# Loading q, k and v as fp32 from the SP queue and casting them on chip, in a windowed attention with a gated FFN behind it

## The chip, the core and the metric

The kernel runs on one core of a Trainium2 chip. Its engines run side by side, each with an instruction stream of its own that it works through in order: PE multiplies matrices, DVE and ACT do elementwise work, Pool does elementwise work too and also issues transfers, and SP does nothing but issue transfers. A transfer that Pool issues can change the type of the data on the way; here, one issued by SP or ACT leaves it as it is. The metric is the time of one execution in microseconds, the median of several runs. One further execution is taken with the profiler, and the views below are of that one.

## The reference

Attention with four sink keys and a window of 128, for 4 batches, 8 heads, 768 positions and head size 64, and behind it an FFN with a gate (512 to 1536 to 512) over all 3072 tokens:

```python
scores = scale * np.matmul(q, k.transpose(0, 1, 3, 2))
keep = (pos[None, :] < 4) | ((rel >= 0) & (rel < 128))      # rel = query - key
a = softmax(np.where(keep, scores, -1e9))
x = np.matmul(a, v).transpose(0, 2, 1, 3).reshape(B * S, H * D)
out = (np.maximum(x @ w_gate, 0.0) * (x @ w_val)) @ w_out
```

## The kernel before

**Tiling.** Work is cut by unit: one batch `b` and one pair of heads `p`, 16 units. The 768 keys of a unit lie in seven tiles of 128 partitions that begin at the rows of `ROW0`. Tiles 1, 3 and 5 carry the four sink keys in their first four partitions, so that the scores of a query need two neighbouring tiles only; tile 6 holds the last 16 rows. q lies in six tiles of 128 rows.

**Loads.** `load_kv` (L87) and `load_q` (L83) issue one transfer a tile from the Pool queue, for both heads at once, and the transfer casts fp32 to bf16 on the way into `kn`, `vn` and `qn`; the sinks are small transfers of their own (L94). A full unit is 26 transfers. There are four slots of these tiles. The weights come in eleven transfers, also from Pool (`load_w`, `load_wo`).

**Stages of a unit.** `st_T` transposes q and k on PE (13 transposes), and DVE, ACT and DVE copy the results out to `qz` and `kT`. `st_S` multiplies scores of one of three column groups, G0, G1 and G2; ACT takes the exponential, DVE multiplies with a 0/1 mask (L170). `st_V` multiplies with v in two parts (rows 0 to 379 and 380 to 767 of the queries), with a row of ones for the denominators, and ACT copies to `oab`. `norm` (L211) sends the denominators to DRAM, back as a dense tile `dc`, through DVE's reciprocal to `dr`, to DRAM again and back, broadcast over 64 partitions, as `R`: four transfers on the SP queue, each of which waits for the one before. Two DVE products with `R` (L233, L234) write the FFN's input `xT`. Steps of `norm` are put off: `tick` counts them down, once after each stage of the prologue and once in each chunk of the FFN.

**The FFN.** `chunk` (L241) makes one of 12 column blocks of the hidden layer for half a batch: four matmuls with `wg`, ACT's relu, four with `wv`, DVE's product to `hT`. `ffn2` (L258) is one of 12 accumulating matmuls of an output tile; ACT copies the tile out, SP stores it.

**Order.** It is written out by hand. The prologue (L274 to L311) loads the first three tiles of batch 0's four units, sets up masks and slots, and runs T, G0, G1a, V part 0 and `norm` of these halves. Then come 8 blocks of 12 chunks (two blocks a batch; the first has 380 columns). Between the chunks the list `stages` is worked off: first the second halves of batch 0, then the 12 full units of batches 1 to 3, T, V part 1 of the unit before, G0, G1, G2, V part 0. `want` (L372) sets how many stages have been issued by each chunk: 2.5 a chunk for 17 chunks, one a chunk after. A unit's loads are issued 11 stages ahead of its T (L357). Three `ffn2` of the block before follow each chunk.

**Buffers.** gp and vp share three PSUM buffers, T, S and V share two (`ps_at`), output tiles have one.

## Time and profile before

| | us |
|---|---|
| median of two runs (463.24 and 463.99) | 463.62 |
| the profiled execution | 466.86 |
| its span, first to last instruction | 465.0 |
| busy in it: Pool | 349.6 |
| PE | 292.8 |
| DVE | 143.7 |
| ACT | 140.8 |

Busy time is summed over the span's instructions of an engine; overlapping matmuls count once. "Pool DMA_DIRECT2D" is the time that Pool takes to issue a transfer, not the transfer's own. In a line of the chain or a timeline the first column is the start in us from the span's start, the second the duration. In a group's line stand count, busy us and mean ns of one, then the idle time of the engine just before and what ended it. A line of windows has: stretch, length, then busy time and count of PE, PE's weight loads, DVE, ACT and Pool, the granted PE clock, the share of time in which the DMA engines were busy, and GB/s.

### The profile page before, as it was taken

What the parts mean: (1) busy time and instruction counts of PE and PEld (TensorE: products, weight loads), DVE (VectorE), ACT (ScalarE), POOL (GpSimd) and SP (SyncE); (2) the same over time, 40 slices, a digit from 0 to 9 for tenths busy, and PEclk for the clock granted to TensorE, in tenths of its full rate; (3) what the DMA queues carried; (4) which work ended last, traced back from release to release, by engine and by line L of the source; (5) the groups of instructions that cost most, each with busy time, mean ns of one, the idle gap of its engine ahead of it and who ended that gap; (6) DMA issues with size and microseconds to landing.
All of it is one profiled execution on the core that took longest, in us unless ns stands there. A gap on an engine that the chain in (4) does not pass through costs nothing.

```text
span 465.0 us, 5011 instructions
## 1 busy us (share of the span) xinstructions
PE 292.8 (63%) x1752; PEld 170.9 (37%) x1752; DVE 143.7 (31%) x280; ACT 140.8 (30%) x225; POOL 349.6 (75%) x439
## 2 busy tenths in 40 slices
PE   0033320564062818254959798897969699999996
PEld 0022110342031505132535354554536365555552
DVE  0721012342022413051624433254334334422220
ACT  1022200353022405051515242433525253233332
POOL 8999499995999999999999999999999400000000
PEclk9999999988557676695979897989889799999999
DMA  4468975659556565756586775768585521110102
GB/s 26 23 33 85 203 63 52 43 45 151 40 33 63 33 66 27 67 42 53 27 90 77 60 88 51 85 45 102 26 90 50 79 52 27 61 47 23 47 23 90
DMA packets 171632, 27.79 MB, mean 60 GB/s; under 512 B 161084, under 2 KB 167756, under 8 KB 171608
## 3 DMA queue, kind: packets, MB, share of 16 engines
q0 software_dynamic: 160944, 14.61, 47.5%
q1 hardware_dynamic: 10664, 12.88, 9.9%
q8 instruction: 13, 0.21, 0.2%
q14 instruction: 11, 0.09, 0.1%
HBM read 34.96 MB, written 6.49 MB: 89 GB/s over the span
## 4 chain that ended last, share of the span: by engine, by line
POOL 61%; PE 23%; DMA 9%; issue 6%; ACT 0%; POOLq 0%; ACTq 0%
POOL vn L92 20%; POOL kn L92 17%; POOL qn L85 13%; PE op L265 8%; PE gp L246 7%; PE vp L252 7%; POOL vn L94 5%; POOL kn L94 4%; DMA kn<-in_k_dram 3%; DMA wo<-in_moe_w_out_dram 2%; DMA qn<-in_q_dram 2%; DMA vn<-in_v_dram 1%; PE ops L181 1%; POOL wg L99 1%; POOL wv L99 1%
## 5 line engine op out<-in xcount | busy, mean ns | idle before, releaser
L92 POOL DMA_DIRECT2D kn<-in_k_dram x112 | 107.4, 968 | 10.5 <-DMA wo<-in_moe_w_out_dram 4.8
L92 POOL DMA_DIRECT2D vn<-in_v_dram x112 | 107.0, 960 | 1.5 <-DMA wg<-in_moe_w_gate_dram 1.1
L144 PE MATMUL tps<-ident,qn 128*128 128x128 bf16 x96 | 23.0, 263 | 126.6 <-DMA qn<-in_q_dram 115.3
L252 PE MATMUL vp<-xT,wv 128*128 128x384 bf16 (+2 forms) x384 | 86.5, 352 | 1.2 <-ACT gs L249 1.2
L246 PE MATMUL gp<-xT,wg 128*128 128x384 bf16 (+2 forms) x384 | 85.7, 349 | 0.0
L265 PE MATMUL op<-wo,hT 128*128 128x512 bf16 x288 | 80.1, 396 | 0.0
L254 DVE TENSOR_TENSOR hT<-gs,vp 128x384 bf16<-128x384 f32 (+2 forms) x96 | 52.4, 547 | 66.9 <-PE vp L252 66.2
L85 POOL DMA_DIRECT2D qn<-in_q_dram x96 | 69.6, 744 | 1.8 <-DMA vn<-in_v_dram 1.1
L152 ACT COPY kT<-tps 128x896 bf16<-128x896 bf16 (+2 forms) x20 | 15.1, 756 | 183.4 <-DVE qz L151 183.4
L144 PEld LDWEIGHTS <-qn 128*128 128x128 bf16 x96 | 9.5, 101 | 142.9 <-DMA qn<-in_q_dram 140.8
L249 ACT ACTIVATE gs<-gp 128x384 f32<-128x384 f32 (+2 forms) x96 | 47.2, 491 | 39.3 <-PE gp L246 38.8
L169 ACT ACTIVATE ee<-sps 128x1014 bf16<-128x1014 f32 (+3 forms) x52 | 45.6, 899 | 25.3 <-PE sps L166 25.2
L252 PEld LDWEIGHTS <-wv 128*128 128x128 bf16 x384 | 40.3, 105 | 31.5 <-issue 9.8
L166 PE MATMUL sps<-qz,kT 128*128 128x255 bf16 (+4 forms) x232 | 31.6, 268 | 23.7 <-DVE qz L151 17.1
L246 PEld LDWEIGHTS <-wg 128*128 128x128 bf16 x384 | 37.2, 103 | 23.3 <-issue 3.7
L170 DVE TENSOR_TENSOR ee<-ee,msk 128x1014 bf16<-128x1014 bf16 (+3 forms) x52 | 31.7, 614 | 39.5 <-ACT ee L169 39.4
L181 PE MATMUL ops<-ee,vn 128*128 128x252 bf16 (+5 forms) x256 | 32.8, 278 | 17.1 <-DVE dr L223 9.2
L151 DVE COPY qz<-tps 64x768 bf16<-64x768 bf16 (+1 forms) x20 | 9.3, 465 | 100.5 <-PE tps L147 100.4
L184 ACT COPY oab<-ops 65x760 f32<-65x760 f32 (+1 forms) x32 | 25.4, 794 | 47.8 <-PE ops L181 47.8
L265 PEld LDWEIGHTS <-hT 128*128 128x128 bf16 x288 | 29.3, 102 | 27.6 <-issue 4.3
L181 PEld LDWEIGHTS <-vn 128*128 128x128 bf16 x256 | 25.6, 116 | 28.7 <-issue 12.8
L166 PEld LDWEIGHTS <-kT 128*128 128x128 bf16 x232 | 22.1, 106 | 36.0 <-DVE qz L151 17.3
(40 smaller groups left out, 163.5 us busy)
## 6 DMA issues: line engine op xcount, KB each, us to landing
out_dram<-ot SPq DMA_DIRECT2D x24, 256.0 KB
R<-rcp_tmp SPq DMA_DIRECT2D x12, 384.0 KB
qn<-in_q_dram POOLq DMA_DIRECT2D x96, 32.0 KB, 2.5
kn<-in_k_dram POOLq DMA_DIRECT2D x48, 32.0 KB, 2.4
vn<-in_v_dram POOLq DMA_DIRECT2D x48, 32.0 KB, 2.5
wg<-in_moe_w_gate_dram POOLq DMA_DIRECT2D x4, 384.0 KB, 9.5
wv<-in_moe_w_val_dram POOLq DMA_DIRECT2D x4, 384.0 KB, 10.7
wo<-in_moe_w_out_dram POOLq DMA_DIRECT2D x3, 512.0 KB, 8.0
```

Of the source, the lines that this page charges most:

```text
L85: nc.gpsimd.dma_start(out=qn[slot][:, t, :, :], in_=rows(q, b, p, t * 128, 128))
L92: nc.gpsimd.dma_start(out=dst[lo:hi, j, :, 0:64], in_=rows(x, b, p, r0 + lo, hi - lo))
L94: nc.gpsimd.dma_start(out=dst[0:4, j, :, 0:64], in_=rows(x, b, p, 0, 4))
L144: nc.tensor.transpose(ps[:, 0, t * 128:(t + 1) * 128], qn[s][:, t, :, :].rearrange("p h d -> p (h d)"), ident[:])
L166: nc.tensor.matmul(out=ps[:, h, c0:c1], lhsT=kT[s][:, j, :], rhs=qz[s][:, h, q0:q0 + c1 - c0], start=True, stop=True)
L169: nc.scalar.activation(e, ps[:, :, lo:hi], Act.Exp, bias=0.0, scale=scale)
L181: nc.tensor.matmul(out=ps[:, h, o0:o0 + c1 - c0], lhsT=vn[s][:, j, h, :], rhs=ee[s][:, gi, h, c0:c1], start=i == 0, stop=i == len(segs) - ...
L246: nc.tensor.matmul(out=gp[:, 0:n], lhsT=wg[:, ko, m * 128:(m + 1) * 128], rhs=x[:, ko, c0:c0 + n], start=ko == 0, stop=ko == KO - 1)
L249: nc.scalar.activation(gs[:, 0:n], gp[:, 0:n], Act.Relu, bias=0.0, scale=1.0)
L252: nc.tensor.matmul(out=vp[:, 0:n], lhsT=wv[:, ko, m * 128:(m + 1) * 128], rhs=x[:, ko, c0:c0 + n], start=ko == 0, stop=ko == KO - 1)
L254: nc.vector.tensor_tensor(hT[:, m, c0:c0 + n], gs[:, 0:n], vp[:, 0:n], op=Alu.mult)
L265: nc.tensor.matmul(out=op, lhsT=hTs[b][:, m, t * 128:(t + 1) * 128], rhs=wo[:, m, :], start=m == 0, stop=m == FM - 1)
```

## The change

- **Loads.** q, k and v are loaded as fp32 into `kf`, `vf` and `qf`, two slots each. A `Unit` issues one transfer per head for k, for q and for v, with all its key tiles in one (they begin 124 rows apart now, so one access pattern covers them and the sinks aren't loaded apart), and one each for the last 24 rows of k and v: eight transfers for a full unit. They are issued from SP; the v of the first halves of batch 0 from ACT. Weights stay on Pool.
- **q's order.** A partition takes `qn` neighbouring rows of q instead of one row of each tile; T's copies to `qz` write with a step of `qn` elements to undo it.
- **Casts.** `cast` copies fp32 to bf16 on chip, with the copies of the sink rows: k, q and v of a unit on Pool, except that k and q of batch 0's first halves are cast on DVE. The `sink` tile keeps batch 0's sink rows for its second halves.
- **Batch 0.** Its units are half units: `P0` (queries 0 to 375) in the prologue, `P1` behind. Two first halves share a slot. There are two slots instead of four in all.
- **Stride.** Key tiles begin every 124 rows; the cuts of the groups and of V move with it (376 and 392 queries instead of 380 and 388), and the masks are built anew.
- **norm.** Its four transfers are put off one by one (`s1` to `s4`), each by one `tick`.
- **Order.** A unit's cast is issued in the second stage of the unit before, its load in the fourth stage of the unit three before. Four stages (`PRE`) are issued ahead of the first chunk; after that two stages a chunk for 18 chunks, then one.

S and V are the same but for offsets. The core of the diff:

```diff
-ROW0 = [0, 124, 252, 376, 504, 628, 752]
-QCUT = 380
+QCUT = 376
...
-    SL = 4
+    kf = [const.tile([128, 7, 2, 64], F32, name=f"kf{i}") for i in range(2)]
+    vf = [const.tile([128, 7, 2, 64], F32, name=f"vf{i}") for i in range(2)]
+    qf = [const.tile([128, 6, 2, 64], F32, name=f"qf{i}") for i in range(2)]
+    sink = const.tile([4, 2, NP, 2, 64], BF16, name="sink")
...
-    def load_q(b, p, ts, slot):
-        for t in ts:
-            nc.gpsimd.dma_start(out=qn[slot][:, t, :, :], in_=rows(q, b, p, t * 128, 128))
-    def load_kv(b, p, js, slot):
-        for x, dst in ((k, kn[slot]), (v, vn[slot])):
-            for j in js:
-                r0 = ROW0[j]
-                lo, hi = (4, 128) if j in (1, 3, 5) else ((0, 16) if j == 6 else (0, 128))
-                nc.gpsimd.dma_start(out=dst[lo:hi, j, :, 0:64], in_=rows(x, b, p, r0 + lo, hi - lo))
-                if j in (1, 3, 5):
-                    nc.gpsimd.dma_start(out=dst[0:4, j, :, 0:64], in_=rows(x, b, p, 0, 4))
...
+    class Unit:
+        def __init__(self, i, b, p, half):
+            self.i, self.b, self.p, self.half, self.s = i, b, p, half, i % 2
+            if half == 0:
+                self.js, self.q0, self.n, self.qn, sub = (0, 1, 2), 0, QCUT, 3, p // 2
+                self.jo, self.qo, self.zo = 3 * sub, 3 * sub, 384 * sub
+                self.qrows, self.qp = 384, 128
+            elif half == 1:
+                self.js, self.q0, self.n, self.qn = (2, 3, 4, 5, 6), QCUT, S - QCUT, 4
+                self.jo, self.qo, self.zo = 0, 0, 0
+                self.qrows, self.qp = S - QCUT, 98
+            else:
+                self.js, self.q0, self.n, self.qn = tuple(range(7)), 0, S, 6
+                self.jo, self.qo, self.zo = 0, 0, 0
+                self.qrows, self.qp = S, 128
+            self.j5 = [j for j in self.js if j < 6]
+            self.a, self.e = self.jo + self.j5[0], self.jo + self.j5[-1] + 1
+        def load(self, eng=None, veng=None):
+            eng, veng = eng or nc.sync, veng or eng or nc.sync
+            s, a, e = self.s, self.a, self.e
+            for en, x, dst in ((eng, k, kf[s]), (eng, q, qf[s]), (veng, v, vf[s])):
+                for h in range(2):
+                    src = x[self.b, 2 * self.p + h]
+                    if x is q:
+                        r = src[self.q0:self.q0 + self.qrows, :].rearrange("(p n) d -> p n d", n=self.qn)
+                        en.dma_start(out=dst[0:self.qp, self.qo:self.qo + self.qn, h, :], in_=r)
+                        continue
+                    r = bass.AP(src.tensor, src.offset + 124 * self.j5[0] * D,
+                                [[D, 128], [124 * D, e - a], [1, D]])
+                    en.dma_start(out=dst[:, a:e, h, :], in_=r)
+                if x is not q and 6 in self.js:
+                    en.dma_start(out=dst[0:24, 6, :, :],
+                                 in_=x[self.b, 2 * self.p:2 * self.p + 2, 744:768, :].rearrange("h s d -> s h d"))
+        def cast(self, what, eng):
+            s, a, e = self.s, self.a, self.e
+            cp = eng.tensor_copy
+            if what == "q":
+                cp(qn[s][0:self.qp, self.qo:self.qo + self.qn, :, :].rearrange("p j h d -> p (j h d)"),
+                   qf[s][0:self.qp, self.qo:self.qo + self.qn, :, :].rearrange("p j h d -> p (j h d)"))
+                return
+            w = 0 if what == "k" else 1
+            src, dst = (kf[s], kn[s]) if w == 0 else (vf[s], vn[s])
+            if w == 0:
+                cp(dst[:, a:e, :, :].rearrange("p j h d -> p (j h d)"),
+                   src[:, a:e, :, :].rearrange("p j h d -> p (j h d)"))
+            else:
+                cp(dst[:, a:e, :, 0:64], src[:, a:e, :, :])
+            if 6 in self.js:
+                cp(dst[0:24, 6, :, 0:64], src[0:24, 6, :, :])
+            if self.half == 0:
+                cp(sink[:, w, self.p, :, :], src[0:4, a, :, :])
+            for j in (1, 3, 5):
+                if j in self.js:
+                    cp(dst[0:4, self.jo + j, :, 0:64],
+                       sink[:, w, self.p, :, :] if self.half == 1 else src[0:4, self.jo, :, :])
+        def T(self):
+            s, nq = self.s, self.qn
+            ps = ps_at.tile([128, 2, 1024], BF16, name="tps", tag="at")
+            w = self.qp * nq
+            po = ps[:, 0, 0:w].rearrange("d (n p) -> d n p", n=nq)
+            for t in range(nq):
+                nc.tensor.transpose(po[:, t, :], qn[s][0:self.qp, self.qo + t, :, :].rearrange("p h d -> p (h d)"),
+                                    ident[0:self.qp, 0:self.qp])
+            for j in self.js:
+                nc.tensor.transpose(ps[:, 1, j * 128:(j + 1) * 128],
+                                    kn[s][:, self.jo + j, :, :].rearrange("p h d -> p (h d)"), ident[:])
+            z0 = self.zo + self.q0
+            d0, d1 = self.js[0], self.js[-1] + 1
+            zq = [qz[s][64 * h:64 * h + 64, h, z0:z0 + w].rearrange("d (p n) -> d n p", n=nq) for h in range(2)]
+            nc.vector.tensor_copy(zq[0], po[0:64])
+            nc.scalar.copy(kT[s][:, self.jo + d0:self.jo + d1, :].rearrange("p j n -> p (j n)"),
+                           ps[:, 1, d0 * 128:d1 * 128])
+            nc.vector.tensor_copy(zq[1], po[64:128])
...
+    def norm(b, p, oab, q0, n, d):
         cc = 12 if n == S else 8
         pp = 2 * n // cc
+        dd, rr = den_d[b, p, 2 * q0:2 * (q0 + n)], rcp_d[b, p, 2 * q0:2 * (q0 + n)]
         dc = dpool.tile([128, 12], F32, name="dc")
         dr = dpool.tile([128, 12], F32, name="dr")
+        R = []
+        def s1():
+            nc.sync.dma_start(out=dc[0:pp, 0:cc], in_=dd.rearrange("(p c) -> p c", c=cc))
+            after(d, s2)
+        def s2():
             nc.vector.reciprocal(dr[0:pp, 0:cc], dc[0:pp, 0:cc])
             nc.sync.dma_start(out=rr.rearrange("(p c) -> p c", c=cc), in_=dr[0:pp, 0:cc])
+            after(d, s3)
+        def s3():
+            R.append(rpool.tile([64, 2, S], F32, name="R"))
+            nc.sync.dma_start(out=R[0][:, :, 0:n], in_=rr.rearrange("(h s) -> h s", h=2).partition_broadcast(64))
+            after(d, s4)
+        def s4():
+            x = xTs[b]
+            busy.discard(next(i for i in range(4) if oab_[i] is oab))
+            ready[b, p] = q0 + n
+            for h in range(2):
+                nc.vector.tensor_tensor(x[64 * h:64 * h + 64, p, q0:q0 + n], oab[0:64, h, q0:q0 + n],
+                                        R[0][:, h, 0:n], op=Alu.mult)
+        nc.sync.dma_start(out=dd.rearrange("(o h s) -> o h s", o=1, h=2), in_=oab[64:65, :, q0:q0 + n])
+        after(d, s1)
...
+        for u in P0:
+            u.load(nc.sync, nc.scalar)
...
+        def cast0(u):
+            u.cast("k", nc.vector)
+            u.cast("q", nc.vector)
+            u.cast("v", nc.gpsimd)
+        def V0(p):
+            o = new_oab()
+            P0[p].V(0, o)
+            norm(0, p, o, 0, QCUT, 1)
+        cast0(P0[0])
+        P0[0].T()
+        cast0(P0[1])
+        P0[1].T()
+        for p in range(NP):
+            P0[p].S("G0")
+            tick()
+            P0[p].S("G1a")
+            tick()
+            if p + 2 < NP:
+                cast0(P0[p + 2])
+                if p == 0:
+                    load_w(0)
+                P0[p + 2].T()
+                if p == 1:
+                    P1[0].load()
+                    P1[1].load()
+            if p >= 1:
+                V0(p - 1)
+            if p == 2:
+                P1[0].cast("k", nc.gpsimd)
+                P1[0].cast("q", nc.gpsimd)
+                load_w(1)
+            if p == 3:
+                P1[0].cast("v", nc.gpsimd)
+            tick()
+        V0(NP - 1)
+        casts(P1[1], nc.gpsimd)
+        P1[2].load()
...
+        def unit_stages(x):
+            u = rest[x]
+            prev = rest[x - 1] if x else None
+            nxt = rest[x + 1] if x + 1 < len(rest) else None
+            nxt3 = rest[x + 3] if x + 3 < len(rest) else None
+            def first():
+                if u.half is None and u.p == 0:
+                    newx(u.b)
+                u.T()
+            yield first
+            if prev is not None:
+                def second():
+                    V_(prev, 1)
+                    if nxt is not None and x >= 1:
+                        casts(nxt, nc.gpsimd)
+                yield second
+            if u.half is None:
+                yield lambda: u.S("G0")
+            yield lambda: u.S("G1" if u.half is None else "G1b")
+            def fourth():
+                u.S("G2")
+                if nxt3 is not None:
+                    nxt3.load()
+            yield fourth
+            if u.half is None:
+                yield lambda: V_(u, 0)
+        for x in range(len(rest)):
+            stages += list(unit_stages(x))
...
+        PRE = 4
+        while si < PRE:
+            stages[si]()
+            si += 1
+            tick()
+        while not all(ready.get((0, p), 0) >= QCUT for p in range(NP)):
+            tick()
         for bi, (b, c0, n) in enumerate(blocks):
             if c0 == 0:
                 hTs[b] = hpool.tile([128, FM, S], BF16, name="hT")
             for m in range(FM):
                 ci = bi * FM + m
-                want = (ci + 1) * 5 // 2 if ci < 17 else 42 + (ci - 16) * 24 // 24
+                want = PRE + (ci + 1) * 2 if ci < 18 else PRE + 38 + (ci - 18)
```

234 lines of the change are left out of this document (74 added, 160 removed), and 8 rows, old and new, of the table SEG.

## The prediction

> **What bounds the kernel now.** I read the page first (span, slices, shares of the chain of waits, costliest groups), then the chain itself, then timelines of PE, SP and DVE, and windows.
>
> ```profile
> span 465.0 us, 5011 instructions
> POOL 8999499995999999999999999999999400000000
> POOL 61%; PE 23%; DMA 9%; issue 6%; ACT 0%; POOLq 0%; ACTq 0%
> L92 POOL DMA_DIRECT2D kn<-in_k_dram x112 | 107.4, 968 | 10.5 <-DMA wo<-in_moe_w_out_dram 4.8
> ```
>
> Pool is full for 31 of 40 slices, it holds 61% of the chain, and what it does is write descriptors: 0.97 us for each small transfer of k, and v and q are loaded the same way. The chain shows the cadence this gives:
>
> ```profile
> 40.34 0.77 POOL wg L99
> ...
> 127.00 4.34 POOL qn L85 x6
> ...
> 148.10 4.34 POOL qn L85 x6
> ...
> 365.18 2.42 DMA qn<-in_q_dram
> ...
> 453.00 8.43 PE op L265 x39
> ```
>
> The q loads of successive units start 21.1 us apart (127.00, 148.10): a unit (one batch, one pair of heads) costs Pool 21.1 us, and twelve of them 253 us. The last q lands at 367.6; only the 97.4 us behind it are PE's own. What PE needs when nothing is late is read where Pool is done:
>
> ```profile
> 375.45 0.60 PE L166 MATMUL sps<-qz,kT 128*128 128x255 bf16 x4
> 375.89 0.81 PE L246 MATMUL gp<-xT,wg 128*128 128x384 bf16 x4
> 376.54 0.81 PE L252 MATMUL vp<-xT,wv 128*128 128x384 bf16 x4
> 377.19 0.81 PE L265 MATMUL op<-wo,hT 128*128 128x512 bf16 x3
> ...
> 380.22 0.54 PE L166 MATMUL sps<-qz,kT 128*128 128x255 bf16 x6
> 380.61 0.81 PE L246 MATMUL gp<-xT,wg 128*128 128x384 bf16 x4
> ...
> 382.56 0.71 PE L181 MATMUL ops<-ee,vn 128*128 128x255 bf16 x6
> 383.11 0.81 PE L246 MATMUL gp<-xT,wg 128*128 128x384 bf16 x4
> ...
> 385.05 0.88 PE L181 MATMUL ops<-ee,vn 128*128 128x127 bf16 x10
> 385.79 0.81 PE L246 MATMUL gp<-xT,wg 128*128 128x384 bf16 x4
> ```
>
> From start to start (matmuls overlap, so the durations don't add): gp 0.65, vp 0.65, a G0 or G1 0.44, a G2 0.39, a V part 0 0.55, a V part 1 0.74. One output matmul is 8.43 / 39 = 0.216 us. Transposes, and the first FFN chunk, in the earlier part of the PE timeline:
>
> ```profile
> 87.23 1.47 PE L246 MATMUL gp<-xT,wg 128*128 128x380 bf16 x4
> ...
> 95.83 0.33 PE L144 MATMUL tps<-ident,qn 128*128 128x128 bf16 x3
> 96.00 0.39 PE L147 MATMUL tps<-ident,kn 128*128 128x128 bf16 x4
> 96.22 1.05 PE L181 MATMUL ops<-ee,vn 128*128 128x127 bf16 x10
> ```
>
> Seven transposes take 0.39 us: 0.056 each.
>
> **PE's whole work from the first chunk on.** 96 chunks x 1.30 = 124.8; 288 output matmuls x 0.216 = 62.2; 12 full units x (13 x 0.056 + 0.44 + 0.44 + 0.39 + 0.55 + 0.74 = 3.29) = 39.5; four second halves of batch 0 x (9 x 0.056 + 0.44 + 0.39 + 0.74 = 2.07) = 8.3. Together 234.8; four stages (1.8 us) now run ahead of the first chunk, so 233. The new stride changes column counts by under 3%: nothing.
>
> **The first chunk's start.** Before it is 87.2 us. Pool's setup no longer stands behind descriptors:
>
> ```profile
> 12.19 0.25 DVE L121 COPY msk<-msk 128x12 bf16<-128x12 bf16 x1 [12.19 <-POOL msk L113]
> ...
> 15.02 0.38 DVE L134 MEMSET qz<- 64x384 uint32 x1
> ...
> 17.12 0.38 DVE L134 MEMSET qz<- 64x384 uint32 x1
> ```
>
> ```profile
> L170 DVE TENSOR_TENSOR ee<-ee,msk 128x1014 bf16<-128x1014 bf16 x28 | 19.4, 692 | 26.7 <-ACT ee L169 26.7
> L233 DVE TENSOR_TENSOR xT<-oab,R 64x768 bf16<-64x768 f32 x12 | 11.4, 950 | 25.5 <-DMA R<-rcp_tmp 25.5
> L111 POOL TENSOR_SCALAR_AFFINE_SELECT msk<-msk 128x252 bf16<-128x252 bf16 x1 | 0.4, 397 | 0.1
> masks.py:199 POOL TENSOR_SCALAR_AFFINE_SELECT ident<-ident 128x128 bf16<-128x128 bf16 x1 | 0.3, 287 | 0.1
> ```
>
> Eight setup operations at no more than 0.40 end at about 3.6 us; DVE's mask work takes 2.8 (12.19 to 15.02), a slot 2.1 (15.02 to 17.12), and there are two slots now: DVE is free at 3.6 + 2.8 + 4.2 = 10.6, and its first casts and the first transposes follow. Before, it took 4.7 us from the last unit's loads (wg starts at 40.34) to that chain's first denominator store (45.06, below). Four half units, one after the other at 4.7, put the first store at 10.6 + 18.8 = 29.4; I take 30, between 20 (two of them hidden) and 45 (as now). From there the order on SP decides:
>
> ```profile
> 45.06 0.71 SPq L217 DMA_DIRECT2D den_tmp<-oab  x1
> ...
> 60.93 0.61 SPq L217 DMA_DIRECT2D den_tmp<-oab  x1
> ...
> 68.01 0.59 SPq L217 DMA_DIRECT2D den_tmp<-oab  x1
> ...
> 79.21 0.62 SPq L226 DMA_DIRECT2D R<-rcp_tmp  x1
> ...
> 381.03 0.34 SPq L270 DMA_DIRECT2D out_dram<-ot  x1
> ```
>
> SP runs its transfers in order, so one pair's store, load, store, broadcast ends before the next pair's begins: 7.1 us a pair (60.93 to 68.01), 11.2 for the last two (to 79.21), 8.0 to the first chunk (87.23). After: 30 + 2 x 7.1 + 11.2 + 8.0 = 63.4. The loads of batch 0's second halves now stand between these on SP: eight each, at 0.34 each at least (the out row, 128 pieces) 2.7 us, mostly in SP's waits: 64. Bounds 53 (from 20) and 87.
>
> **Loads.** The 26 Pool transfers of a unit become eight on SP: (6 x 128 x 2 + 48) x 2 + 6 x 128 x 2 = 4704 rows of 256 bytes.
>
> ```profile
> q0 software_dynamic: 160944, 14.61, 47.5%
> q1 hardware_dynamic: 10664, 12.88, 9.9%
> ```
>
> No row shows such a transfer. From below: q1's time per byte, 0.099 x 465 x 16 / 12.88 MB = 57 us a MB, is 15 ns a row. From above: all of q0's time on its 74,752 rows of q, k, v (counted from the loops) is 47 ns. I take 20, near q1: the same kind of queue, without a cast. A unit's load is then 4704 x 20 / 16 = 5.9 us of the engines (4.3 to 13.8). SP's issue of one is between 0.34 and six times that, 2.0 (768 pieces against 128); I take 0.7, so 5 us a unit. In the steady part a unit has six chunks of 1.30 + 0.65 and its own 3.29: 15.0 us. The load stands behind that unit's four norm transfers, and the next denominator store comes three stages, 7.5 us, later. Both fit: no cost. If not, what is late next is the denominator, see the first rival.
>
> The Trainium skill (DMA: Bandwidth & Descriptors, Specifications) speaks against this: below 512 bytes a transfer does a read-modify-write and misses line rate. If I price that as twice the bytes' 15 ns, an estimate, a unit's load is 8.8 us, over the 7.5, and the sum grows by 1.3 x 12 = 16 us.
>
> **Casts on Pool.** Three of 768 elements and eight small ones a unit. Bounds from the two affine_select rows: 0.89 ns an element (397 less 287, over 124) and 0.17 fixed. Big 0.85, small 0.29: 3 x 0.85 + 8 x 0.29 = 4.9 us; from 1.9 (fixed only) to 7.8 (twice the slope for fp32). The casts are issued four stages before the transposes that read them, some 10 us: hidden, so Pool costs nothing. A cast waits for its load and for V of the unit two back; SP's load three units ahead waits for the cast that frees its fp32 tile, and behind it on SP stand the next denominators and out stores. DVE's qz copies write with a step: at worst 0.95, the 768-element row, hidden by the two chunks before G0.
>
> **Stalls.** Two stages a chunk run in the first 18 chunks. Windows:
>
> ```profile
> 87.00:111.00 24.00, 17.98 (x137) 11.62 (x136) 8.78 (x19) 12.81 (x20) 23.63 (x30) 0.93 0.71 74
> 380.00:410.00 30.00, 28.84 (x176) 16.42 (x175) 12.31 (x21) 11.20 (x21) 0.00 (x0) 1.00 0.22 62
> ```
>
> In the first, of this kind, PE idles 25%; the part after holds about 47 us of PE work, so 47 x 24 / 17.98 - 47 = 16 at most, partly waits on loads: I take 10. The second idles 4%: over some 136 us of steady work 5.5. The end, last matmul to end of span, is 465.0 - 461.4 = 3.6.
>
> **Sum.** 64 + 233 + 10 + 5.5 + 3.6 = 316 us of span. The profiled execution took 466.86 for its span of 465.0 (+1.9), and stands 3.2 above the median of 463.62: about 315.
>
> **Rivals.**
> - *SP and the DMA rings take Pool's place.* At 47 ns a row, or 2.0 us an issue, a load lasts 13 us, 5.5 more than the 7.5 until the next denominator. DVE waits in order for it at the reciprocal, behind it the mask and hT products, then PE. 5.5 x 12 = 66: 381. For it: one SP queue now carries everything. Against: q1 shows 15 ns for the bytes.
> - *Pool's casts hold up DVE.* Five DVE products a unit read two SBUF tiles (rows L170, L233). If each waited for one 0.85 us cast and nothing hid it, 5 x 0.85 x 12 = 51: 366; half of them, 341. No row shows Pool reading while DVE multiplies. The Trainium skill (SBUF — State Buffer, Who interferes with whom) states that a Vector instruction with two SBUF inputs contends with a GpSimd one that reads SBUF, under an exclusive lock. Against: DVE has slack in each chunk.
> - *Slower: the casts are as dear as the descriptors.* One mechanism: Pool stays the bound when a unit's casts exceed (473 - 64 - 28 - 97) / 12 = 23.7 us, with 28 for batch 0's second halves and 97 for the end as before. At 25 us it gives 489. It needs five times my 4.9; then the change would not do what it says, and just under it is no change.
> - *All hidden.* First chunk at 53 and no early stalls: 315 - 11 - 10 = 294; I count it with the forecast.
>
> **How the numbers follow.** Forecast 0.67 (own range 285 to 345), SP and rings 0.19, Pool against DVE 0.08, casts too dear 0.04, casts just under that 0.02. Range 285 to 355: it leaves out the first rival's upper two thirds (0.13) and the last two (0.06). 2% is about what a measurement can tell: faster 0.94, within 2% 0.02, slower 0.04.
>
> **What would show it.** Pool's slices fall to some 3 tenths; the chain is PE after the first chunk; gp begins near 64; SP's den to dc stays near 2 us in the steady part. Wrong if DVE's waits on dc grow past 5 us a unit, if Pool casts exceed 2 us, or if PE waits for kn or qn casts.

## The result, and the profile after

The changed kernel takes 390.44 us (median of two runs, 390.11 to 390.76) for 463.62 before: a ratio of 0.842, with an interval of 0.838 to 0.846. The forecast was faster, 315 us with a range of 285 to 355: the direction holds, the size does not, 75 us are missing. In the tables below, the ratios leave out executions that took over 1.5% more than the fastest of their kernel, the medians do not (two of four with the old row order and weights late, one of four with the old row order and R from Pool).

The page of the changed kernel: span, Pool's row of the forty slices, the queue that now carries the loads, the chain that ended last by engine.

```profile
span 388.4 us, 5029 instructions
POOL 6240531307424304311404040404010000000000
q1 hardware_dynamic: 87208, 31.91, 37.5%
PE 48%; DVE 24%; DMA 11%; ACT 6%; issue 4%; SPq 4%; POOL 1%; DVEq 0%; ACTq 0%; POOLq 0%
```

Pool was busy through 31 slices and held 61% of the chain; now it is mostly idle and holds 1%. That bound is gone. But DVE, absent from the chain before, has 24% of it. The groups by line, shapes kept apart, of DVE, and its waits and PE's over the whole run:

```profile
L156 DVE COPY qz<-tps 64x768 bf16<-64x768 bf16 x12 | 32.7, 2724 | 11.7 <-ACT kT L154 11.7
L153 DVE COPY qz<-tps 64x768 bf16<-64x768 bf16 x12 | 32.6, 2714 | 3.5 <-PE tps L148 3.5
```

```profile
PE sps L164 <- DVE qz L156: 39.5, 17, 5.7
DVE xT L287 <- DMA R<-rcp_tmp: 34.1, 14, 6.9
```

A copy of 768 columns of q from PSUM to `qz` takes 2.72 us, and PE waits 39.5 us for the second of the two before it can multiply scores. Windows (width, then busy time of PE, PEld, DVE, ACT and Pool, granted clock, DMA share, GB/s) by part:

```profile
98.00:171.00 73.00, 47.99 (x325) 30.67 (x322) 54.98 (x57) 30.38 (x43) 22.96 (x57) 0.80 0.53 114
191.00:313.00 122.00, 108.77 (x745) 65.39 (x744) 82.62 (x96) 58.25 (x94) 18.92 (x49) 0.98 0.41 88
313.00:385.00 72.00, 70.63 (x392) 37.90 (x389) 20.39 (x37) 22.50 (x45) 0.00 (x0) 1.00 0.13 47
```

PE idles 2% of the last stretch, 11% of the steady part with one stage a chunk, and 34% of the part with two stages a chunk. Ahead of these the FFN's first matmul comes at 79.0 us (first start in the row of its tile), where 64 was forecast:

```profile
L301 PE MATMUL gp<-xT,wg x384: 319/326/534, 79.0 to 375.4; 128*128 128x384 bf16 x144, 128*128 128x376 bf16 x24, 128*128 128x392 bf16 x24
```

So three places are to be explained: the copies, the prologue, and the part with two stages a chunk. PE's granted clock, 0.80 in the first of these windows, comes back in the account of the prediction.

### The profile page after: what moved, and what is told of

Read it like the earlier page. It is cut to its first block, busy times and chain, and to the rows that moved or that the text cites. A ratio compares the mean times of both kernels' runs of the same rounds, so it can differ in the third digit from the quotient of the medians.

```text
span 388.4 us, 5029 instructions
## 1 busy us (share of the span) xinstructions
PE 272.5 (70%) x1760; PEld 163.6 (42%) x1760; DVE 207.7 (53%) x286; ACT 141.3 (36%) x225; POOL 83.2 (21%) x203
## 2 busy tenths in 40 slices
DMA packets 96241, 37.74 MB, mean 97 GB/s; under 512 B 85692, under 2 KB 92364, under 8 KB 96216
## 4 chain that ended last, share of the span: by engine, by line
PE 48%; DVE 24%; DMA 11%; ACT 6%; issue 4%; SPq 4%; POOL 1%; DVEq 0%; ACTq 0%; POOLq 0%
PE vp L307 14%; PE op L320 13%; PE gp L301 12%; DVE qz L153 10%; DVE qz L156 8%; PE sps L164 6%; DMA kf<-in_k_dram 4%; ACT kT L154 3%; DMA R<-rcp_tmp 3%; DMA dc<-den_tmp 2%; DVE xT L287 2%; PE ops L176 2%; ACT ee L167 2%; SPq L109 2%; SPq L111 1%
## 5 line engine op out<-in xcount | busy, mean ns | idle before, releaser
L307 PE MATMUL vp<-xT,wv 128*128 128x384 bf16 (+2 forms) x384 | 83.2, 342 | 14.2 <-ACT gs L304 14.2
L164 PE MATMUL sps<-qz,kT 128*128 128x251 bf16 (+5 forms) x232 | 35.3, 293 | 47.8 <-DVE qz L156 39.5
L167 ACT ACTIVATE ee<-sps 128x1006 bf16<-128x1006 f32 (+4 forms) x52 | 46.1, 900 | 53.2 <-PE sps L164 53.2
L168 DVE TENSOR_TENSOR ee<-ee,msk 128x1006 bf16<-128x1006 bf16 (+4 forms) x52 | 33.8, 651 | 39.4 <-ACT ee L167 38.8
L287 DVE TENSOR_TENSOR xT<-oab,R 64x768 bf16<-64x768 f32 (+2 forms) x40 | 33.2, 830 | 34.4 <-DMA R<-rcp_tmp 34.1
L128 POOL CAST vn<-vf 128x768 bf16<-128x768 f32 (+2 forms) x20 | 14.7, 732 | 165.8 <-PE ops L176 163.1
L156 DVE COPY qz<-tps 64x768 bf16<-64x768 bf16 (+2 forms) x20 | 40.0, 2000 | 17.1 <-ACT kT L154 17.1
L176 PE MATMUL ops<-ee,vn 128*128 128x248 bf16 (+6 forms) x256 | 28.6, 255 | 25.8 <-DVE ee L168 18.1
L153 DVE COPY qz<-tps 64x768 bf16<-64x768 bf16 (+2 forms) x20 | 39.8, 1990 | 7.3 <-PE tps L148 7.2
L179 ACT COPY oab<-ops 65x752 f32<-65x752 f32 (+1 forms) x32 | 25.4, 795 | 25.5 <-PE ops L176 25.3
L145 PE MATMUL tps<-ident,qn 128*128 128x128 bf16 (+1 forms) x100 | 9.8, 236 | 18.5 <-DVE qn L119 18.3
L324 ACT COPY ot<-op 128x512 f32<-128x512 f32 x24 | 14.1, 587 | 22.2 <-PE op L320 22.2
```

The source lines that it names most:

```text
L153: nc.vector.tensor_copy(zq[0], po[0:64])
L156: nc.vector.tensor_copy(zq[1], po[64:128])
L164: nc.tensor.matmul(out=ps[:, h, c0:c1], lhsT=kT[s][:, self.jo + j, :], rhs=qz[s][:, h, self.zo + q0:self.zo + q0 + c1 - c0], start=True, s ...
L167: nc.scalar.activation(x, ps[:, :, lo:hi], Act.Exp, bias=0.0, scale=scale)
L168: nc.vector.tensor_tensor(x, x, msk[:, gi, :, lo:hi], op=Alu.mult)
L176: nc.tensor.matmul(out=ps[:, h, o0:o0 + c1 - c0], lhsT=vn[s][:, self.jo + j, h, :], rhs=ee[s][:, gi, h, c0:c1], start=i == 0, stop=i == le ...
```

## The experiments

Times are medians on the chip; a ratio is to the kernel before, run beside it, with its interval.

| kernel | us | ratio |
|---|---|---|
| changed kernel | 390.4 | 0.842 (0.838 to 0.846) |
| q in the old row order | 362.2 | 0.779 (0.777 to 0.781) |
| copies that read with the step | 365.9 | 0.785 (0.779 to 0.791) |
| weights late | 390.8 | 0.843 (0.839 to 0.847) |
| old row order, weights late | 361.3 | 0.772 (0.769 to 0.774) |
| Pool's large casts twice | 396.2 | 0.854 (0.851 to 0.856) |
| kernel before with the stepped copies | 465.9 | 1.000 (0.998 to 1.003) |
| old row order, R from Pool | 362.7 | 0.782 (0.776 to 0.787) |
| old row order, weights early | 355.5 | 0.764 (0.759 to 0.768) |
| read with the step, weights early | 364.9 | 0.783 (0.778 to 0.788) |
| read with the step, weights early, R from Pool | 362.5 | 0.778 (0.773 to 0.784) |
| read with the step, weights early, loads behind R | 372.7 | 0.800 (0.793 to 0.807) |

The rest, on the old row order with early weights (355.5), stand in the last part below.

### The stepped copies

**q in the old row order.** The copies write in one piece again; nothing else moves.

```diff
-  r = src[self.q0:self.q0 + self.qrows, :].rearrange("(p n) d -> p n d", n=self.qn)
+  r = bass.AP(src.tensor, src.offset + self.q0 * D, [[D, self.qp], [self.qp * D, self.qn], [1, D]])
...
-  zq = [qz[s][64 * h:64 * h + 64, h, z0:z0 + w].rearrange("d (p n) -> d n p", n=nq) for h in range(2)]
+  zq = [qz[s][64 * h:64 * h + 64, h, z0:z0 + w] for h in range(2)]
...
```

> The changed kernel with one part undone: q is loaded with neighbouring rows in neighbouring partitions, as before, in the same number of transfers and of 256-byte pieces, so that DVE's two copies to qz write without a step. Theory A (the stepped copies, 2.72 us each where 0.95 was the assumed worst, hold up DVE, G0 and the hT products behind them): the copies fall to about 0.55 us, PE's waits on qz before G0 (5 to 6 us a unit in the part with two stages a chunk) go, and the time falls by 35 to 55 us, to 335 to 355. Theory B (transfers in one another's way on SP and the DMA engines): the copies get shorter but the time falls by no more than 8 us, to 382 or more. Theory C (Pool's casts late, or in DVE's way): no more than 8 us either.

362.2 us: 28 less, short of the 35 to 55, but the largest single gain of all runs on complete kernels. One of its two copies (0.55 us; the other takes 0.56), and its windows:

```profile
L154 DVE COPY qz<-tps 64x768 bf16<-64x768 bf16 x12 | 6.5, 546 | 1.9 <-PE tps L149 1.9
```

```profile
92.00:175.00 83.00, 56.57 (x418) 37.70 (x421) 44.28 (x71) 36.90 (x55) 33.36 (x74) 0.89 0.63 128
175.00:290.00 115.00, 109.91 (x763) 68.63 (x776) 57.95 (x99) 59.99 (x97) 19.34 (x49) 0.99 0.45 96
290.00:355.00 65.00, 64.06 (x350) 34.67 (x355) 18.22 (x32) 20.10 (x39) 0.00 (x0) 1.00 0.13 47
```

In the steady part PE now idles 4%, as forecast. The part before it still idles 32%: that loss has another cause.

**The kernel before with the stepped copies.** q comes in the changed kernel's row order, still by Pool's transfers, and the copies write with the step; everything else is as before.

```diff
...
+  r = rows(q, b, p, ts[0] * 128, 128 * n).rearrange("(p n) h d -> p n h d", n=n)
+  nc.gpsimd.dma_start(out=qn[slot][:, t, :, :], in_=r[:, t - ts[0]])
...
+  zq = [qz[s][64 * h:64 * h + 64, h, c0:c1].rearrange("d (p n) -> d n p", n=nq) for h in range(2)]
...
```

> The kernel before with the stepped copies alone: q is loaded in the changed kernel's row order, and DVE puts the transposed columns back in order with copies that write with a step; all else, Pool's loads too, is as before. Theory A (the dear copies are what the changed kernel loses): each copy of 768 columns takes 2.7 us here too instead of 0.55, but Pool's descriptor writing, 21 us a unit, still sets the pace, so DVE's extra 4 to 6 us a unit is hidden: ratio 0.995 to 1.015. Rival: the copies are dear only where Pool casts beside them (the two hold one another up at the SBUF port): 0.55 to 0.95 us each here.

```profile
L158 DVE COPY qz<-tps 64x768 bf16<-64x768 bf16 x12 | 32.7, 2721 | 11.7 <-ACT kT L157 11.7
```

The same 2.72 us, with no cast on Pool, and the time does not change: a ratio of 1.0004. The copies are dear by themselves, and under the old bound they were free. Their 28 us in the changed kernel exist only because Pool no longer covers them.

**Copies alone.** Each form three times, with zeros stored as output ahead of them.

> No part of the reference is computed: copies of 64 x 768 bf16 alone, each form three times, on DVE: PSUM to SBUF with writes 1, 2, 3, 4, 6, 8, 12 and 16 elements apart; in the kernel's form with 2, 3, 4 and 6 tiles; a stepped read of PSUM with a write in one piece; a stepped write from SBUF; the same on ACT. From the changed kernel's rows, an element costs about 1.8, 2.4 and 3.4 ns at 6, 8 and 12 bytes apart. Theory by lines (a dear step whenever the next element lies in another 16-byte line): the cost is level from 16 bytes on, about 3.6 us a copy at 8, 12 and 16 elements apart; 4 bytes apart about 1.0 us. Theory by extent (the cost grows with the bytes passed over): 4.6 ns an element at 16 bytes, 9 ns at 32: 3.6, 5.3 and 7.1 us at 8, 12 and 16 elements apart. A write in one piece with a stepped read: 0.55 us if only the write side is dear, 2.7 if both are. ACT: as DVE if the port is the reason; 0.7 to 0.9 us if DVE alone is.

Groups by line of this run (the lines 55 to 69 are writes 1, 2, 3, 4, 6, 8, 12 and 16 elements apart; 77 is the kernel's own form with six tiles, 79 reads PSUM with the step and writes in one piece, 81 writes with the step from SBUF, 83 and 85 are ACT with a step of 6 and without):

```profile
L65 DVE COPY dst<-ps 64x768 bf16<-64x768 bf16 x3 | 10.6, 3542 | 0.1
L67 DVE COPY dst<-ps 64x768 bf16<-64x768 bf16 x3 | 10.5, 3509 | 0.1
L69 DVE COPY dst<-ps 64x768 bf16<-64x768 bf16 x3 | 10.0, 3350 | 0.1
L83 ACT COPY das<-ps 64x768 bf16<-64x768 bf16 x3 | 8.1, 2699 | 0.1
L63 DVE COPY dst<-ps 64x768 bf16<-64x768 bf16 x3 | 8.1, 2695 | 0.1
L77 DVE COPY dst<-ps 64x768 bf16<-64x768 bf16 x3 | 8.1, 2695 | 0.1
...
L61 DVE COPY dst<-ps 64x768 bf16<-64x768 bf16 x3 | 5.5, 1846 | 0.1
...
L81 DVE COPY dst<-sb 64x768 bf16<-64x768 bf16 x3 | 4.3, 1434 | 0.1
L59 DVE COPY dst<-ps 64x768 bf16<-64x768 bf16 x3 | 4.3, 1424 | 0.1
...
L57 DVE COPY dst<-ps 64x768 bf16<-64x768 bf16 x3 | 3.0, 1005 | 0.1
...
L79 DVE COPY dst<-ps 64x768 bf16<-64x768 bf16 x3 | 2.8, 949 | 0.1
L85 ACT COPY das<-ps 64x768 bf16<-64x768 bf16 x3 | 2.4, 792 | 0.1
L55 DVE COPY dst<-ps 64x768 bf16<-64x768 bf16 x3 | 1.6, 550 | 1.0 <-PE ps L53 0.9
```

From 4 to 12 bytes apart the price grows by (2695 - 1005) / 8 = 211 ns for a byte; at 16 it is 3542, and at 24 and 32 no more. Theory by lines fits these rows, theory by extent (7.1 us at 32 bytes) falls. The Trainium skill (SBUF — State Buffer, Specifications (TRN2)) states that SBUF has lines of 16 bytes, wants two hits or more a line for full speed, and that each cross to a new line pays; the level above 16 bytes agrees, but here the price grows from 4 to 6 to 8 bytes apart (1005, 1424 and 1846 ns), where a line still takes two hits or more, and the measurement decides. The rise from 550 to 1005 may be a matter of its own, for a stepped read that is written in one piece takes 949 too; these rows don't tell the two apart. At 12 bytes ACT pays as much as DVE.

**Copies that read with the step.** The changed kernel with the step on the other side: PSUM is read with it, `qz` is written in one piece.

```diff
-  zq = [qz[s][64 * h:64 * h + 64, h, z0:z0 + w].rearrange("d (p n) -> d n p", n=nq) for h in range(2)]
-  nc.vector.tensor_copy(zq[0], po[0:64])
+  zq = [qz[s][64 * h:64 * h + 64, h, z0:z0 + w].rearrange("d (p n) -> d p n", n=nq) for h in range(2)]
+  pr = po.rearrange("d n p -> d p n")
+  nc.vector.tensor_copy(zq[0], pr[0:64])
...
```

> The changed kernel with one expression turned round: the q copies write in one piece and read PSUM with the step (0.95 us in the run of copies alone, against 2.70). Loads, casts and order are the changed kernel's. Theory A: the same as with q in the old row order (362.2 us), or better by what the larger pieces of q save on the rings (1.5 KB instead of 256 B): 352 to 364, ratio 0.76 to 0.785. Rival (the old row order helped in another way than through the copies): 375 to 391.

```profile
L154 DVE COPY qz<-tps 64x768 bf16<-64x768 bf16 x12 | 11.4, 946 | 3.4 <-PE tps L148 3.4
```

365.9 us, a little over the 352 to 364 expected, with copies of 0.95 us: 25 of the 28 by an edit that leaves the loads alone, so it is the copies and not the row order. (The expectation's larger pieces do not exist: the page counts 96242 packets here and 96241 with the old row order.)

**Pool's casts.** Each large cast on Pool is done twice.

> The changed kernel with every large cast on Pool done twice (the second copy writes the same values again): some 2.5 us more Pool time in each full unit, 43 us over the span with the half units. Theories A and B: Pool is hidden, and the time stays within 1% of 390. Theory C: if Pool's casts were on the path, each full unit would grow by up to 2.5 us, 30 us in all, to about 420; a part of that if they only get in the way of DVE's products with two inputs in SBUF.

Pool's busy time grows from 83.2 to 124.6 us, the kernel's by 5.7 (ratio 0.854 for 0.842). Some six sevenths of the added casts are hidden. The rest is a little more than the 1% of theories A and B and far less than the 30 us of theory C, which is no main cause. What the casts do hold up is DVE's products with two inputs in SBUF: the largest of the mask products (128x1006) takes 0.955 us on average, 0.744 in the changed kernel; the copies from PSUM take 2.72 to 2.73 in both.

### The weights in the prologue

In the changed kernel DVE waits 14.1 us, until 70.9, for the way back of a denominator, while the last weights and a half unit's loads are under way. **Weights late** puts `load_w(2)` and `load_w(3)` behind the casts of the second stage of P1's second unit, and `load_wo` a unit later; the second kernel does this on the old row order.

> The changed kernel with the last seven weight transfers moved: the two last quarters of wg and wv are issued by Pool behind the casts in the second stage of the second half unit, wo behind those of the third; nothing else is changed. Theory B (the seven weight transfers, issued together at 47 to 52 us, stand in front of the loads of batch 0's third second half and of the denominators of the last two pairs, for which DVE waits 14.1 us at a reciprocal): that wait falls to about 2 us, the first FFN chunk starts at 64 to 69 instead of 79 us, and the time falls by 9 to 14 us, to 376 to 381. Theory A: the chunks' part is bound by the stepped copies and takes 306 us again; it says nothing of the prologue. Theory C: no change.

> Both edits together: q's old row order and the weights issued later. Theories A and B, each for its own part of the span, make the two gains add up: 35 to 55 and 9 to 14 us, a time of 322 to 346. If one cause lay behind both, the sum would fall clearly short of the two single gains.

No gain on the changed kernel: 390.8 us. On the old row order it is 361.3 for 362.2, by the ratios (0.772 for 0.779) some 3 us; neither is the 9 to 14 us expected. The timeline of DVE with late weights shows the wait gone from one place and come back at another (the bracket is the wait before the instruction):

```profile
57.48 0.20 DVE L273 RECIPROCAL dr<-dc 94x8 f32<-94x8 f32 x1 [1.79 <-DMA dc<-den_tmp]
60.81 1.10 DVE L287 TENSOR_TENSOR xT<-oab,R 64x376 bf16<-64x376 f32 x2 [2.66 <-DMA R<-rcp_tmp]
75.47 1.10 DVE L287 TENSOR_TENSOR xT<-oab,R 64x376 bf16<-64x376 f32 x2 [10.68 <-DMA R<-rcp_tmp]
```

The first chunk does start at 65.5 us instead of 79.0, as expected, but it needs the products at 75.47 as well, and the second starts at 79.7 instead of 85.1. These 5 us are lost again by the nineteenth chunk, the first with one stage: 167.0 for 166.9. So in the changed kernel the date of the first chunk doesn't set the time.

**Weights early** issues them ahead of the stages instead:

```diff
   if p == 1:
+      load_w(1)
+      load_w(2)
       P1[0].load()
...
-      load_w(1)
+      load_w(3)
```

(`wo` goes behind the cast of v at `p == 3`.)

> On top of q in the old row order (362.2 us): the FFN weights' transfers are issued earlier, w1 and w2 in front of stage 1, w3 in front of stage 2, wo in front of stage 3 of the prologue, so that none stands between the first denominators and their way back. Theory B: the wait for dc of 13.9 us at 69.6 falls under 5, the first chunk starts at 66 instead of 76, time 350 to 354, ratio 0.755 to 0.765. Rival: as with the late weights, the wait moves (the loads of stages 1 to 3 come later by what the weights take): 360 to 364.

> The copies read with the step, and the weights' transfers are issued early, as in e7_w_early. If the two add up as they did on q in the old row order (6.6 us): 346 to 358, ratio 0.745 to 0.77. Rival: the prologue's transfers were late by q's small pieces, which are gone, so the early weights bring nothing: within 1.5 us of e9.

355.5 us on the old row order, 6.6 less; but 364.9 on the copies that read with the step, 0.9 less. In the second, DVE waits 13.13 us for its first denominator, until 43.2 us, and the first chunk starts at 78.7, no earlier than without the edit (77.9): there the wait moved once more. What makes the difference between the two was not tried.

### The part with two stages a chunk

Three edits that were to bring R sooner:

> On top of q in the old row order (362.2 us): the broadcast of the reciprocals, R, is issued from Pool's queue instead of SP's, where it stands behind a unit's loads. Theory D (R stands behind loads, in SP's queue and on the rings): DVE's waits for R in the part with the half units (23 us from 92 to 175 us) fall under 6, time 345 to 350, ratio to the kernel before 0.74 to 0.755. Rival: R is late because the transfers before it have to land on the same engines, whoever issues it, or the wait moves to the next thing: 358 to 364, ratio 0.77 to 0.785.

> As e10, and R issued from Pool's queue. From e6 (no gain on q in the old row order): within 3 us of e10. If it was q's small pieces on the rings that kept R late there, the gain of 10 us or more shows here.

> As e10, but a unit's loads are issued after the R (and the reciprocals' write) of the same place in the order, one chunk later for whole units and two for half units. Theory D (R stands behind loads on the rings): DVE's waits for R up to 175 us fall by half, time 5 to 12 us under e10. Rival: the wait moves to the casts of the units whose loads now come later, or the part is bound by something else: within 2 us of e10.

362.7, 362.5 and 372.7 us. **R from Pool** (`nc.gpsimd.dma_start` for the broadcast) brings nothing: now Pool stands, 30.6 us in five waits from 76 to 175 us in the first of them, until the reciprocals are in memory, and its casts with it. **Loads behind R** (`after(1, ...)` and `after(2, ...)` around a unit's load) costs 8 us: Pool's k casts wait 23.1 us for the loads there, and DVE still waits 29.0 for R. Theory D falls in this form.

The next four kernels are built on the old row order with early weights (355.5 us).

> On q in the old row order with early weights (355.5 us): the q loads of the whole units are left out (these units compute with an older q), a third of the rows that a unit loads. Theory T (from 75 to 165 us the transfers' own time sets the pace): a chunk there takes 4.3 us for the 2.6 of the later part; with a third of the load gone about 0.7 us less for each of 18 chunks, 340 to 346. Theory W (DVE's in-order wait for R sets it): R lands sooner only by what stands ahead of it, 347 to 353.

> On the same kernel: the broadcast of the reciprocals is left out and the products take a constant of ones (no division by the denominators); denominators, reciprocals and their own transfers stay. Theory W: 325 to 338. Theory T: R is about a third of a unit's transfers in time, 338 to 346. If a rival is right by which the stages' own chain (exp, mask, copies) sets the pace of two stages a chunk: 350 to 356.

> As e14, but R is broadcast all the same and nobody reads it: the transfer stays and the wait goes. Theory W: within 4 us of e14, 325 to 340. Theory T: little, 348 to 356.

> On the same kernel, complete: the products that need R stand two places behind its issue instead of one, so that DVE comes to them a chunk later. Theory W: the waits for R up to 175 us fall by more than half, 335 to 347. Rival: the later products hold up the first chunk of each block, or the wait moves to the loads: 351 to 358.

| | us | ratio |
|---|---|---|
| no q loads of whole units | 346.5 | 0.743 (0.738 to 0.748) |
| no R | 321.1 | 0.689 (0.687 to 0.692) |
| R moved, unread | 345.4 | 0.742 (0.738 to 0.745) |
| products a place later | 351.8 | 0.755 (0.752 to 0.759) |

"No R" and "R moved, unread" leave out the division by the denominators, as does "R of other memory" below; they are there to measure with. Without q's loads the time falls between the ranges of theories T and W, which decides nothing. DVE's wait for R alone is worth 355.5 - 345.4 = 10 us, not the 20 of theory W, and nearly all of it is one wait that lies behind the 18 chunks with two stages: the nineteenth chunk comes 0.7 us sooner, the end of the span 9.0 (table below). There R is issued behind a unit's eight loads, and DVE stands for it, with hT behind (early weights; DVE's line, then SP's):

```profile
163.36 1.91 DVE L288 TENSOR_TENSOR xT<-oab,R 64x768 bf16<-64x768 f32 x2 [9.56 <-DMA R<-rcp_tmp]
```

```profile
152.44 0.32 SPq L275 DMA_DIRECT2D rcp_tmp<-dr  x1
152.85 0.97 SPq L110 DMA_DIRECT2D kf<-in_k_dram  x2
...
159.51 0.45 SPq L280 DMA_DIRECT2D R<-rcp_tmp  x1
```

Within the 18 chunks the wait only moves: with R unread, DVE waits 23.0 us from 76 to 165 us for denominators. With the products a place later, its waits for R there fall from 25.1 to 6.3 us, but 7.0 come back behind, until 166.5, where the first chunk of batch 1 waits for the products: the rival.

Taking R away as well gives 24 us more than R unread, more than theory T's bytes, and 321.1 is below every range expected. That pointed to SP's own queue. Its timeline in the kernel with early weights, one turn for each unit (start, time of the issue):

```profile
110.37 0.63 SPq L280 DMA_DIRECT2D R<-rcp_tmp  x1
111.10 0.39 SPq L291 DMA_DIRECT2D den_tmp<-oab  x1
113.30 0.35 SPq L270 DMA_DIRECT2D dc<-den_tmp  x1
113.74 1.02 SPq L110 DMA_DIRECT2D kf<-in_k_dram  x2
114.81 0.50 SPq L112 DMA_DIRECT2D kf<-in_k_dram  x1
115.41 0.95 SPq L106 DMA_DIRECT2D qf<-in_q_dram  x2
116.46 1.08 SPq L110 DMA_DIRECT2D vf<-in_v_dram  x2
117.58 0.75 SPq L112 DMA_DIRECT2D vf<-in_v_dram  x1
118.44 0.34 SPq L275 DMA_DIRECT2D rcp_tmp<-dr  x1
121.38 0.47 SPq L280 DMA_DIRECT2D R<-rcp_tmp  x1
121.95 0.39 SPq L291 DMA_DIRECT2D den_tmp<-oab  x1
125.06 0.33 SPq L270 DMA_DIRECT2D dc<-den_tmp  x1
```

From R to R 11.0 us. SP issues for some 6 of them; it stands 1.8 (111.49 to 113.30) until the denominators have landed and 2.6 (118.78 to 121.38) until the reciprocals have, and the next unit's loads stand behind. By the prediction's prices PE needs 3 x 1.30 + 3.29 = 7.2 us for that unit and its three chunks.

**R of other memory** is built on "R moved, unread" and moves R's bytes from a place that nobody writes, so that SP need not wait:

```diff
-  in_=rr.rearrange("(h s) -> h s", h=2).partition_broadcast(64)
+  in_=k[b, 2 * p].rearrange("s d -> (s d)")[0:2 * n].rearrange("(h s) -> h s", h=2).partition_broadcast(64)
```

**SP waits nowhere** is complete: each step of `norm` that needs a landing is issued a chunk later (`s1`, `s3` and `s4` by `after(2, ...)`).

> As e15 (R broadcast and unread, products by a constant of ones: no division), but the broadcast reads other memory, so that the same bytes move and SP's queue doesn't stand until the reciprocals' write has landed (16.6 us in 7 waits from 76 to 165 us in e15). Theory Q (SP's queue is one loop there: a unit's loads, the wait for the reciprocals, R, the wait for the denominators): 328 to 337, nearer to the 321.1 without R. Theory T (the bytes of R on the rings are what costs): 341 to 347, as e15.

> A complete kernel, as e16 (351.8 us), and the read of the denominators and the broadcast R are issued a place later too, so that what SP waits for has landed by then. Theory Q: SP's waits for the two writes (26 us from 76 to 165 us) fall under 8, time 335 to 345. Theory T: 349 to 354. Rival: the chain from denominators to products, two chunks longer, comes late for the blocks' first chunks: 352 to 365.

327.9 us (0.706, 0.702 to 0.709) and 345.1 us (0.742, 0.739 to 0.746). With all of R's bytes moved, the first comes to within 7 us of the kernel without R: theory Q. The second is 10.4 below the kernel with early weights and the fastest complete one, 45 us below the changed kernel; it lies at the upper end of theory Q's range. SP's waits in it from 76 to 165 us:

```profile
SPq L275 <- DVE dr L274: 18.1, 7, 5.5
...
SPq L280 <- DMA rcp_tmp<-dr: 2.8, 2, 2.6
...
SPq L270 <- DMA den_tmp<-oab: 0.7, 1, 0.7
```

The waits for the two landings are down from 22.9 us (13.0 and 9.9 with early weights) to 3.5, as expected. But SP now waits 18.1 us in the same stretch for DVE's reciprocals, so that in this complete kernel most of the wait has moved. The windows from 76 to 165 us of the kernel with early weights and of this one, in separate fences:

```profile
76.00:165.00 89.00, 63.54 (x503) 43.87 (x502) 45.76 (x79) 41.71 (x62) 40.05 (x87) 0.94 0.68 138
```

```profile
76.00:165.00 89.00, 68.19 (x520) 44.95 (x518) 51.83 (x86) 46.36 (x68) 40.91 (x87) 0.90 0.63 130
```

PE gets through 3% more matmuls in the same stretch (520 for 503), at a lower granted clock. Where each kernel gains is seen by the starts of its chunks (us from the start of the span, from gp's matmuls in the profiled execution; the first 18 chunks have two stages each):

| kernel | first | second | nineteenth | end of span |
|---|---|---|---|---|
| changed kernel | 79.0 | 85.1 | 166.9 | 388.4 |
| weights late | 65.5 | 79.7 | 167.0 | 388.5 |
| q in the old row order | 76.3 | 82.6 | 151.1 | 358.9 |
| old row order, weights early | 71.7 | 78.1 | 145.8 | 352.3 |
| R moved, unread | 70.0 | 74.0 | 145.1 | 343.3 |
| R of other memory | 66.5 | 70.6 | 131.3 | 328.4 |
| no R | 62.4 | 65.9 | 125.4 | 319.4 |
| SP waits nowhere | 65.0 | 75.5 | 140.4 | 343.6 |

From "R moved, unread" to "R of other memory" the second chunk comes 3.4 us sooner, the nineteenth 13.8, the end 14.9: most of what SP's standing costs lies where theory Q has it. For "SP waits nowhere" against early weights the three are 2.6, 5.4 and 8.7 us: it gains less than 3 us in the part that it was made for, and about as much before it and behind it. So theory Q is shown by the kernels without the division; that a complete kernel can have these 17.5 us back is not shown.

## Why the prediction was wrong

**The bound that goes: right.** Pool's 21.1 us a unit are gone, and its casts cost what the sum had for them (0.85 for a large one, 0.29 for a small one), by the groups of the changed kernel:

```profile
L135 POOL CAST vn<-vf 4x128 bf16<-4x128 f32 x40 | 11.1, 305 | 0.0
L125 POOL CAST kn<-kf 128x768 bf16<-128x768 f32 x12 | 10.7, 890 | 4.1 <-DMA kf<-in_k_dram 4.1
```

**PE's whole work: counted right, but at the full clock.** The rows that priced it (from 375 us of the kernel before) lie where the granted clock was 1.00, and the sum has no term for a lower one. From the first chunk on PE is busy 253.8 us in the changed kernel, at a mean clock of 0.93, where 233 were forecast; with q in the old row order it is 243.6 at 0.96, without R 235.6 at 0.98. All these kernels multiply the same matrices. What lowers the clock was not tried: in the changed kernel it is 0.80 to 0.84 from 98 to 191 us, where PE stands a third of the time, but 1.00 in the prologue, where it stands more. The steady stalls are right once the copies are out: PE then idles 4% of the steady part.

**Price of the loads: right.** The hardware queue (packets, MB, share of 16 engines' span) with early weights, span 352.3 us, and without the q loads of the whole units, span 344.2:

```profile
q1 hardware_dynamic: 87208, 31.91, 41.6%
```

```profile
q1 hardware_dynamic: 68392, 27.19, 35.0%
```

18816 packets fewer, and 146.6 - 120.5 = 26.1 us less on each of 16 engines: 22 ns a row, 20 was taken. The doubling that the prediction drew, as an estimate, from the Trainium skill (DMA: Bandwidth & Descriptors, Specifications) would be 30; these rows don't show it, though 22 is more than the 15 of the bytes. A load's issue takes 0.5 us (4.3 for the eight in the timeline above) where 0.7 was taken.

**"At worst 0.95, the 768-element row": the first step that failed.** That row was a product of the same size that writes in one piece; its price says nothing of a step. The copy takes 2.72. "Hidden by the two chunks before G0" failed with it: two such copies with ACT's between them are longer than two chunks of 1.30 with their stages. Price: 28 us, about half between the second and the nineteenth chunk and half behind.

**"Both fit: no cost": the second.** The 7.5 us until the next denominator were worked out for the steady part, with six chunks a unit. In the first 18 chunks a unit has three, and there a unit's turn of SP's queue is 11 us. The prediction said that SP works in order and that loads "stand behind that unit's four norm transfers". In the steady part of the changed kernel they do (R at 235.06, the loads from 235.63 on); in this part they stand between `dc` and the reciprocals' store (113.74 to 118.3 in the timeline above), and at 152.85, just behind the part, between that store and R. It put no number on SP standing still. It took 10 us for all stalls of this part from a window of the kernel before, in which the loads were on another queue; from the first to the nineteenth chunk PE stands 29.8 us in the changed kernel and still 20.0 with q in the old row order. Run by run: 10 us for DVE's wait for R, nearly all of it the wait of 9.56 behind this part; 345.4 - 327.9 = 17.5 for SP's standing until the reciprocals have landed, some of it in the prologue; 327.9 - 321.1 = 6.8 for R's bytes and issue.

**The weights, not costed.** "Weights stay on Pool" in the change had no term in the sum; they stand against the prologue's loads and denominators, and the first chunk starts at 79.0 instead of 64. Late weights bring it to 65.5 and the time not at all; early weights bring 6.6 us on one base and 0.9 on another. So this term is the least certain, and what the late first chunk costs by itself stays open.

**The sum.** 28 + 6.6 + 10 + 17.5 + 6.8 = 69 of 75 us, each measured on top of the one before; in another order the parts would differ. In the prediction's own terms, the span of 388.4 us for 316 is 15 more before the first chunk, 21 more of PE's busy time (253.8 for 233) and 36.5 more of standing behind that (55.6 for 19.1). The kernel without R takes 321 us, 6 over the forecast, and its terms are near the forecast's: 62.4, 235.6 and 21.4. It leaves out a transfer that the forecast counted; with R's bytes moved it is 328. So the forecast was near to what the kernel takes when little is late, and wrong in what is late.

**The rivals.** SP as the new bound came true in part: not by dear rows or dear issues, as it was priced, but by standing in order, and most of all in the part with two stages a chunk. Its 381 us lies near the 390 measured by luck: it has no stepped copies in it. Pool's casts against DVE, priced at 26 to 51 us, did not come true at that price: doubling them costs 5.7. The slower rival did not.

## What to carry to other kernels

When a bound goes, list what ran under it and price each piece by a row of its own form: a copy that costs nothing before can be the next bound, and a row of the same size with another access pattern is no bound for it. Put a step on the side that reads, or into the transfer, rather than on the side that writes. When transfers are gathered on one queue, add up its turn: the issues and every landing that the queue waits for in order, in the part of the schedule where a unit has the least time; then issue what depends on a landing later, rather than from another queue that does other work, and look where the wait goes: here that brought 10 us in a complete kernel, but most of SP's standing moved to its wait for DVE.

## What the runs showed of the hardware

- A bf16 copy from PSUM to SBUF of 64 x 768 takes 0.55 us in one piece and 1.01, 1.42, 1.85, 2.70 and 3.54 us when it writes 4, 6, 8, 12 and 16 bytes apart, and no more beyond; ACT's takes 2.70 at 12 bytes for 0.79. The same write from SBUF takes 1.43, and reading PSUM with the step 0.95.
- A transfer of 768 pieces of 256 bytes takes SP about 0.5 us to issue, and the engines about 22 ns a piece.
- A small store and the load that reads it back hold the queue that issues both for 2.0 to 2.2 us on average, 2.7 at most, where a unit's loads are under way (early weights, 76 to 165 us: 13.0 us in 6 waits, 9.9 in 5).
- Large casts done twice on Pool bring one of DVE's products of two SBUF tiles (masks, 128x1006) from 0.744 to 0.955 us on average; the one of 128x830 stays at 0.602, and the stepped copies from PSUM at 2.72 to 2.73.
